# DCN-v2 cross layers on one core: the last round's row blocks stored one by one, the last block's store divided between two queues

## Chip, cores and metric

The kernel runs on one NeuronCore of a Trainium2 chip. The metric is the device time of one execution in microseconds (us). A core has five engines with instruction streams of their own: TensorE (PE; its weight loads are PEld), VectorE (DVE), ScalarE (ACT), GpSimd (POOL) and SyncE (SP), which here does nothing but issue DMA transfers. DMAs are issued by SP and by ScalarE, each into a queue of its own (SPq and ACTq in the profile's rows). KB is 1024 bytes.

## What is computed

Six cross layers over a batch of 4096 rows of 416 features, all in bfloat16:

```python
B, F, D, L = 4096, 26, 16, 6
Din = min(F * D, 1024)          # 416
# x0: [4096, 416], ws: [6, 416, 416], bs: [6, 416]
def reference(x0, ws, bs):
    x = x0
    for l in range(ws.shape[0]):
        x = x0 * (x @ ws[l] + bs[l]) + x
    return x
```

## The kernel before

Every x is x0 times a factor c, with c = 1 at the start and c + (x @ W + b) after each layer. So the kernel keeps c, adds each layer's product to it, and multiplies by x0.

**First five layers.** Activations lie transposed: features on partitions, batch rows along the free dimension. The 416 features are three chunks of 128 (XM0, XH, CM) and a remainder of 32 (XR, CR), the batch two halves `s` of 2048 rows. TensorE multiplies into PSUM tiles (`pt`), ScalarE evicts them with the bias (L187, L333), VectorE adds into CM and multiplies by XM0. In the fifth layer (`feeding_layer`) c is also sent through DMA transposes on SP (L232, L380), so that it lies with batch rows on partitions in XLrows. X0rows is x0 in the same layout; SP loads it early (L131 to L133), behind the weights, in 18 transfers of one or two row blocks each. Four loads of the last bias follow it on SP (L135), and then the transposes.

**Last layer (from L446).** Its product comes out with batch rows on partitions. A *row block* is 128 rows by 416 columns, one PSUM bank of 416 float32 per partition, 104 KB in bfloat16. There are 32 row blocks, worked off in four rounds of eight (`rounds`, L518). In a round a block has a number `u` from 0 to 7. When `mm_q_full` has finished a block or two, `close` calls `ew`. There ScalarE copies the bank to an SBUF tile `t` (L507), and VectorE adds the rows of XLrows (L511). The product with X0rows (L494) and the store wait in the list `pending` until the next block's addition has been put in VectorE's stream; `close_product` then writes the product into an output tile `o` and issues the store. Output tiles hold two blocks and come from a pool of ten (`opool`).

**Last round.** Here blocks are closed one at a time, in order (`ENDS`). `final` is true and three things differ. For u of 5 and more c was added on TensorE with an identity (L468, L470), so that L511 is left out. Block 7 isn't copied by ScalarE either: VectorE's product reads it in PSUM (L494, `o<-py`). And `paired` (L528) decides how blocks share output tiles and stores: blocks 0 to 5 lie two in a tile, `j` being 0 or 1, and each tile is stored when its second block is there (`last`). Blocks 6 and 7 have a tile and a store each. All stores are issued by SP, only block 7's by ScalarE (`eng`, L532).

**What orders the work.** VectorE's instructions and some others are pinned in program order. Each engine runs its stream in order; between engines the framework puts semaphore waits. SP issues its stores in order, each behind a wait for VectorE's product. The end sequence (L577) waits on SP for the stores to land, and then all engines meet at a barrier.

Of the kernel before, what the change touches and what calls it, by code (L numbers as in the profile page):

```python
# [16 lines left out]
def kernel(  # L17
# [7 lines left out]
    nc = tc.nc  # L25
    B, D = x0.shape
    L = ws.shape[0]
    P = 128
# [7 lines left out]
    NBT = B // P  # L36
# [9 lines left out]
    out_v = out.rearrange("(bt p) d -> p bt d", p=P)  # L46
# [26 lines left out]
    def load_wm(eng, l):  # L73
        eng.dma_start(WM[:, l], ws[l, 0:NK * P, :].rearrange("(k p) n -> p k n", p=P))
# [5 lines left out]
    def pin(ins):  # L80
        tc.keep_in_program_order(ins)
# [46 lines left out]
        load_wr(nc.sync, g, 1, L)  # L128
    for l in range(2, L):
        load_wm(nc.sync, l)  # L130
    for q in range(18):  # L131
        b0, b1 = NBT * q // 18, NBT * (q + 1) // 18
        nc.sync.dma_start(X0rows[:, b0:b1, :], x0_v[:, b0:b1, :])  # L133
    for g in range(NG):
        nc.sync.dma_start(bLr[32 * g:32 * g + 1, :], bs[LL:LL + 1, :])  # L135
# [319 lines left out]
    def mm_q_open(q, g, py):  # L455
        for k in range(NK):
            for j in range(0, P, 32):
                nc.tensor.matmul(py[j:j + 32, 0:D], lhsT=q_x(q, g, k)[:, j:j + 32], rhs=WM[:, l, k, :],  # L458
                                 start=(k == 0), stop=False, tile_position=(0, j))

    def mm_q_full(q, g, py, closes, adds=False):
        s, i = quads[q]
        for k in range(NK):
            nc.tensor.matmul(py[:, 0:D], lhsT=q_x(q, g, k), rhs=WM[:, l, k, :],  # L464
                             start=((not closes) and k == 0), stop=(closes and not adds and k == NK - 1))
            if adds:
                c0 = col0(s, g) + 128 * i
                nc.tensor.matmul(py[:, P * k:P * k + P], lhsT=CM[:, k, c0:c0 + 128], rhs=ident[:], start=False, stop=False)  # L468
        if adds:
            nc.tensor.matmul(py[:, NK * P:D], lhsT=CR[:, CW * s + 128 * i:CW * s + 128 * i + 128],  # L470
                             rhs=ident[:, 32 * g:32 * g + 32], start=False, stop=True)

    def mm_q_rem(q, py, done):
        s, i = quads[q]
        biased = s == NS - 1 and i >= 2
        for g in range(NG):
            nc.tensor.matmul(py[g][:, 0:D], lhsT=curR[32 * g:32 * g + 32, CW * s + 128 * i:CW * s + 128 * i + 128],  # L477
                             rhs=WR[32 * g:32 * g + 32, l, :], start=(g >= done), stop=(not biased and g < done),
                             tile_position=(32 * g, 0))
        for g in range(NG if biased else 0):  # L480
            nc.tensor.matmul(py[g][:, 0:D], lhsT=ones[32 * g:32 * g + 1, :],  # L481
                             rhs=bLr[32 * g:32 * g + 1, :], start=False, stop=(g < done), tile_position=(32 * g, 0))

    pending, outs = [], []

    def rows(q, g0, n):
        s, i = quads[q]
        b0 = 16 * s + 4 * g0 + i
        return slice(b0, b0 + 4 * (n - 1) + 1, 4)

    def close_product():
        while pending:
            src, q, g0, n, o, j, last, eng = pending.pop()
            pin(nc.vector.tensor_tensor(out=o[:, j:j + n, :], in0=src, in1=X0rows[:, rows(q, g0, n), :], op=ALU.mult))  # L494
            if last:
                eng.dma_start(out_v[:, rows(q, g0 - j, j + n), :], o[:, 0:j + n, :])

    def ew(q, g0, srcs, o, j, last, eng, added, direct):
        if direct:
            close_product()  # L500
            pending.append((srcs[0], q, g0, 1, o, j, last, eng))
            return
        t = tpool.tile([P, 2 * CW], BF16, name="t")
        n = 0
        for src in srcs:
            w = src.shape[1]
            nc.scalar.copy(t[:, n * D:n * D + w * D].rearrange("p (a d) -> p a d", a=w), src)  # L507
            n += w
        tv = t[:, 0:n * D].rearrange("p (a d) -> p a d", a=n)
        if not added:  # L510
            pin(nc.vector.tensor_tensor(out=tv, in0=tv, in1=XLrows[:, rows(q, g0, n), :], op=ALU.add))  # L511
        close_product()
        pending.append((tv, q, g0, n, o, j, last, eng))
# [5 lines left out]
    for q, at, done in rounds:  # L519
        tiles = [psum.tile([P, 2, CW], FP32, tag="ps", name=f"py{n}") for n in range(4)]  # L520
        bank = [tiles[n][:, a, :] for n, a in at]

        final = q + 2 == NQ

        def close(groups):
            u = groups[0][0]
            srcs = [tiles[at[g[0]][0]][:, at[g[0]][1]:at[g[0]][1] + len(g), 0:D] for g in groups]
            paired = final and u < 6  # L528
            j = u % 2 if paired else 0
            if not j:  # L530
                outs.append(opool.tile([P, 2, D], BF16, name="o"))
            ew(q + u // 4, u % 4, srcs, outs[-1], j, bool(j) or not paired, nc.scalar if final and u == 7 else nc.sync,  # L532
               final and u >= 5, final and u == 7)

        for u in range(done):
            if q == 0:
                mm_q_open(q, u, bank[u])
            else:
                mm_q_full(q, u, bank[u], False)
        mm_q_rem(q, bank[0:4], done)  # L540
        close([range(done)])
        if q == 0:
            last_rows_out()
        mm_q_rem(q + 1, bank[4:8], 0)
        for u in range(done, 8):
            mm_q_full(q + u // 4, u % 4, bank[u], True, final and u >= 5)
            if at is ENDS:
                close([[u]])
            elif u % 2:
                close([[u - 1, u]] if at is PAIRS else [[u - 1], [u]])  # L550
    close_product()


# [28 lines left out]
```

## Time and profile before

| | us |
|---|---|
| median of 3 runs | 128.86 (128.81 to 128.91) |
| the profiled execution's own time | 129.12 |
| its span, first to last instruction | 127.3 |
| TensorE clock granted | 1.000 |
| last layer begins (first L458 in the chain of waits) | 103.6 |
| last matmul (L470) starts | 123.65 |
| product of block 7 on VectorE (L494, from PSUM) | 123.97, lasts 0.58 |

The span leaves out what lies around the program's instructions, so a change of the span stands beside the same change of the time. In the profile's rows "L494 DVE ... o<-t,X0rows 128x416" is an instruction of line 494 on VectorE that writes `o` and reads `t` and `X0rows`; a trailing number after x counts instructions. In the timeline a row of several instructions shows the first one's start and the time until the last one's end. Some rows of the stage around the change:

```profile
L464 PE MATMUL py<-WM,XH 128*128 128x416 bf16 x90 | 17.0, 339 | 0.0
L494 DVE TENSOR_TENSOR o<-t,X0rows 128x832 bf16<-128x832 bf16 x12 | 7.0, 584 | 0.0
L507 ACT CAST t<-py 128x416 bf16<-128x416 f32 x13 | 6.6, 506 | 1.6 <-PE py L481 0.6 <-PE py L464 0.4 <-DVE o L494 0.2
L494 DVE TENSOR_TENSOR o<-t,X0rows 128x416 bf16<-128x416 bf16 x7 | 2.4, 372 | 0.1
L494 DVE TENSOR_TENSOR o<-py,X0rows 128x416 bf16<-128x416 f32 x1 | 0.6, 584 | 0.0
...
out_dram<-o SPq DMA_DIRECT2D x15, 208.0 KB, 2.9
X0rows<-in_x_dram SPq DMA_DIRECT2D x14, 208.0 KB, 4.4
X0rows<-in_x_dram SPq DMA_DIRECT2D x4, 104.0 KB, 5.4
out_dram<-o SPq DMA_DIRECT2D x1, 104.0 KB
```

In the first five rows the two numbers after the bar are busy us of all and mean ns of one, and after the second bar stands the engine's idle time before them. The other rows are DMA issues: how many, KB of each, and the median us from issue to landing.

### The profile page before, as it was taken

Reading aid. Unit: us, or ns where it says so; the run is one execution under the profiler, and the core shown is the slowest. Engines: PE = TensorE matmul, PEld = TensorE weight load, DVE = VectorE, ACT = ScalarE, POOL = GpSimd, SP = SyncE. Lnnn points to the kernel's source line nnn. Section 1 sums busy time; section 2 is a strip of 40 time slices with the busy share of each in tenths; the row PEclk is TensorE's granted clock in tenths of the full one; section 3 lists DMA queues with packets and bytes.
Section 4 is the critical chain, followed back from the end, with each engine's and each line's share of the span. In section 5 each row is a group of like instructions: output and inputs, shape, how many; then the busy total and the mean of one; then the engine's idle time right before and its main releaser. Section 6 shows DMA issues by size and latency. Waiting matters only on the chain.

```text
span 127.3 us, 3951 instructions
## 1 busy us (share of the span) xinstructions
PE 122.9 (97%) x1684; PEld 55.3 (43%) x1686; DVE 102.4 (80%) x192; ACT 88.3 (69%) x113; POOL 5.1 (4%) x18
## 2 busy tenths in 40 slices
PE   7999999999999999999999999999999999999980
PEld 3243343344534443444354445444534445445450
DVE  0033679674989898998898998898999999999991
ACT  0047866896869486869486859485859698679660
POOL 4004001400000000000000000000000000000000
PEclk9999999999999999999999999999999999999999
DMA  3999999999960000000000000000088999999865
GB/s 90 239 222 228 190 242 256 299 332 335 315 192 0 5 0 0 8 0 5 0 5 0 0 5 0 5 0 5 0 83 137 197 150 202 171 256 320 262 198 187
DMA packets 42230, 16.38 MB, mean 129 GB/s; under 512 B 31034, under 2 KB 42212, under 8 KB 42212
## 3 DMA queue, kind: packets, MB, share of 16 engines
q1 hardware_dynamic: 37432, 15.40, 53.3%
q10 hardware_dynamic: 4780, 0.72, 3.7%
q8 instruction: 13, 0.21, 0.7%
q14 instruction: 5, 0.04, 0.1%
HBM read 6.15 MB, written 3.41 MB: 75 GB/s over the span
## 4 chain that ended last, share of the span: by engine, by line
PE 90%; DMA 5%; SPq 1%; DVEq 1%; ACT 0%; issue 0%; DVE 0%
PE pt L209 50%; PE py L464 12%; PE ph L241 11%; DMA XM<-in_x_dram 5%; PE pt L215 5%; PE pr L225 5%; PE pr L221 2%; PE py L477 2%; PE ph L248 1%; SPq L78 1%; PE py L458 1%; DVEq L577 1%; ACT t L507 0%; PE py L481 0%; PE py L468 0%
## 5 line engine op out<-in xcount | busy, mean ns | idle before, releaser
L209 PE MATMUL pt<-XH,WM 128*32 128x512 bf16 x1152 | 65.2, 379 | 0.0
L187 ACT ACTIVATE t<-pt,bM 128x1024 bf16<-128x1024 f32 x36 | 37.2, 1115 | 13.1 <-PE pt L215 13.1
L209 PEld LDWEIGHTS <-WM 128*32 128x32 bf16 x1152 | 29.7, 97 | 33.8 <-issue 5.1
L188 DVE TENSOR_TENSOR CM<-t,CM 128x1024 bf16<-128x1024 bf16 x36 | 24.7, 687 | 4.3 <-ACT t L187 4.3
L189 DVE TENSOR_TENSOR XH<-CM,XM 128x1024 bf16<-128x1024 bf16 x36 | 24.9, 692 | 2.6
L507 ACT CAST t<-py 128x416 bf16<-128x416 f32 (+1 forms) x22 | 14.2, 649 | 4.2 <-PE py L464 2.0
L464 PE MATMUL py<-WM,XH 128*128 128x416 bf16 x90 | 17.0, 339 | 0.0
L241 PE MATMUL ph<-XM,WM 128*128 128x512 bf16 x70 | 16.3, 380 | 0.2
L333 ACT ACTIVATE t<-pt,bM 128x1024 bf16<-128x1024 f32 x12 | 12.4, 1115 | 4.1 <-PE pt L215 4.1
L181 ACT ACTIVATE CM<-ph,bM 128x1024 bf16<-128x1024 f32 x12 | 12.5, 1114 | 3.5 <-PE ph L248 3.5
L183 DVE TENSOR_TENSOR XH<-CM,XM 128x512 bf16<-128x512 bf16 x24 | 8.9, 430 | 4.5 <-ACT CM L181 4.5
L464 PEld LDWEIGHTS <-XH 128*128 128x128 bf16 x90 | 8.5, 98 | 7.5 <-issue 1.2
L241 PEld LDWEIGHTS <-WM 128*128 128x128 bf16 x72 | 6.7, 98 | 8.6 <-issue 1.3
L494 DVE TENSOR_TENSOR o<-t,X0rows 128x832 bf16<-128x832 bf16 (+1 forms) x19 | 9.4, 506 | 0.1
L511 DVE TENSOR_TENSOR t<-t,XLrows 128x832 bf16<-128x832 bf16 (+1 forms) x17 | 8.9, 523 | 0.0
L341 DVE TENSOR_TENSOR CM<-t,CM 128x1024 bf16<-128x1024 bf16 x12 | 8.0, 686 | 0.3 <-ACT t L333 0.3
L345 DVE TENSOR_TENSOR XH<-CM,XM 128x2048 bf16<-128x2048 bf16 (+1 forms) x7 | 7.5, 1068 | 0.2
L215 PE MATMUL pt<-XR,WR 32*128 32x512 bf16 x96 | 7.3, 379 | 0.0
L225 PE MATMUL pr<-XH,WM 128*32 128x512 bf16 x96 | 6.6, 379 | 0.0
L197 ACT ACTIVATE t<-pr,bR 128x256 bf16<-128x256 f32 (+1 forms) x16 | 5.3, 427 | 1.6 <-PE pr L225 1.6
L114 ACT ACT_TABLE_LOAD x1 | 1.3, 1283 | 6.1 <-DMA XM<-in_x_dram 6.1
L157 DVE CAST bM<-pb 128x18 f32<-128x18 bf16 x1 | 0.2, 177 | 5.5 <-PE pb L156 5.5
(61 smaller groups left out, 62.2 us busy)
## 6 DMA issues: line engine op xcount, KB each, us to landing
out_dram<-o SPq DMA_DIRECT2D x15, 208.0 KB, 2.9
X0rows<-in_x_dram SPq DMA_DIRECT2D x14, 208.0 KB, 4.4
WM<-in_ws_dram SPq DMA_DIRECT2D x5, 312.0 KB, 5.7
WR<-in_ws_dram SPq DMA_DIRECT2D x4, 130.0 KB, 3.9
X0rows<-in_x_dram SPq DMA_DIRECT2D x4, 104.0 KB, 5.4
WM<-in_ws_dram ACTq DMA_DIRECT2D x1, 312.0 KB, 3.3
XM<-in_x_dram SPq DMA_TRANSPOSE x8, 5.1
xrig<-in_x_dram ACTq DMA_DIRECT2D x4, 32.0 KB, 4.5
```

The source lines that it names most:

```text
L181: nc.scalar.activation(c, src, ACT.Identity, bias=bias, scale=1.0)
L187: nc.scalar.activation(t[:], src, ACT.Identity, bias=bias, scale=1.0)
L188: nc.vector.tensor_tensor(out=c, in0=t[:], in1=c, op=ALU.add)
L189: nc.vector.tensor_tensor(out=x, in0=c, in1=XM0[:, m, c0:c0 + 2 * CW], op=ALU.mult)
L209: nc.tensor.matmul(pts[g // 2][32 * q:32 * q + 32, g % 2, :], lhsT=WM[:, l, k, 128 * m + 32 * q:128 * m + 32 * q + 32], rhs=cur[s][:, k, C ...
L215: nc.tensor.matmul(pts[g // 2][:, g % 2, :], lhsT=WR[32 * g:32 * g + 32, l, 128 * m:128 * m + 128], rhs=curR[32 * g:32 * g + 32, CW * s:CW ...
L225: nc.tensor.matmul(pr[32 * g:32 * g + 32, :], lhsT=WM[:, l, k, NK * P:D], rhs=cur[s][:, k, CW * g:CW * g + CW], start=False, stop=(k == NK ...
L241: nc.tensor.matmul(pt[:, gl, :], lhsT=WM[:, 0, k, 128 * m:128 * m + 128], rhs=cur[:, k, c0:c0 + CW], start=(k == 0 and not after_row), sto ...
L333: nc.scalar.activation(ts[t + (h,)][:], pts[t][h][:].rearrange("p a b -> p (a b)"), ACT.Identity, bias=bM[:, t[1], l:l + 1], scale=1.0)
L464: nc.tensor.matmul(py[:, 0:D], lhsT=q_x(q, g, k), rhs=WM[:, l, k, :], start=((not closes) and k == 0), stop=(closes and not adds and k == ...
L494: pin(nc.vector.tensor_tensor(out=o[:, j:j + n, :], in0=src, in1=X0rows[:, rows(q, g0, n), :], op=ALU.mult))
L507: nc.scalar.copy(t[:, n * D:n * D + w * D].rearrange("p (a d) -> p a d", a=w), src)
```

## The change

X0rows comes in 15 loads of two or three row blocks (104 KB a block) instead of 18 of one or two. In the last round only blocks 4 and 5 still share a tile and a store; blocks 0 to 3 have a tile and a store each. Block 7's store becomes two: SP issues partitions 0 to 63, ScalarE partitions 64 to 127, 52 KB each. A block with `eng` set to `None` is block 7.

```diff
-    for q in range(18):
-        b0, b1 = NBT * q // 18, NBT * (q + 1) // 18
+    for q in range(15):
+        b0, b1 = NBT * q // 15, NBT * (q + 1) // 15
         nc.sync.dma_start(X0rows[:, b0:b1, :], x0_v[:, b0:b1, :])
...
             pin(nc.vector.tensor_tensor(out=o[:, j:j + n, :], in0=src, in1=X0rows[:, rows(q, g0, n), :], op=ALU.mult))
-            if last:
+            if eng is None:
+                for e, part in ((nc.sync, slice(0, P // 2)), (nc.scalar, slice(P // 2, P))):
+                    e.dma_start(out_v[part, rows(q, g0, 1), :], o[part, 0:1, :])
+            elif last:
                 eng.dma_start(out_v[:, rows(q, g0 - j, j + n), :], o[:, 0:j + n, :])
...
-            paired = final and u < 6
+            paired = final and u in (4, 5)
             j = u % 2 if paired else 0
             if not j:
                 outs.append(opool.tile([P, 2, D], BF16, name="o"))
-            ew(q + u // 4, u % 4, srcs, outs[-1], j, bool(j) or not paired, nc.scalar if final and u == 7 else nc.sync,
+            ew(q + u // 4, u % 4, srcs, outs[-1], j, bool(j) or not paired, None if final and u == 7 else nc.sync,
                final and u >= 5, final and u == 7)
```

## The prediction

> **What bounds the kernel now.** I read the page's engine sums and chain first, then the chain's last pieces, the waits of SP's queue, SP's and ScalarE's timeline of the last microseconds, the DMA issues, and last a table of short stretches from 121 us on.
>
> ```profile
> span 127.3 us, 3951 instructions
> PE 122.9 (97%) x1684; PEld 55.3 (43%) x1686; DVE 102.4 (80%) x192; ACT 88.3 (69%) x113; POOL 5.1 (4%) x18
> ...
> 123.68 0.04 DVE o L494
> 123.72 0.16 issue
> 123.88 0.68 DVEq L577
> ```
>
> TensorE is busy 97% of the span, and the chain is almost all TensorE until 123.1 us. The change touches nothing on TensorE. The listed chain ends at 123.88 + 0.68 = 124.56 us, though the span ends at 127.3: the last 2.7 us belong to something the chain doesn't follow. The waits of SP's queue show what:
>
> ```profile
> SPq L577 <- DMA out_dram<-o: 1.8, 4, 0.6
> ...
> 123.07 0.94 SPq L496 DMA_DIRECT2D out_dram<-o  x2
> 123.64 0.90 SPq L496 DMA_DIRECT2D out_dram<-o  x2
> ...
> 124.59 0.38 ACTq L496 DMA_DIRECT2D out_dram<-o  x1
> ...
> out_dram<-o ACTq DMA_DIRECT2D x1, 104.0 KB, 1.9
> DMA to landing us min/median/max: 1.9/2.7/3.6
> ```
>
> At its end (L577) SP waits four times for stores. The last store, ScalarE's 104 KB, is issued at 124.59 and lands 1.9 us later, at 126.5; the end sequence takes the other 0.8 us to 127.3. So the end is the landing of the last store, and only what moves that landing counts. Here is what the DMA engines do then (last two columns: busy share of the 16 engines, GB/s):
>
> ```profile
> 122.40:122.60 0.20, 0.20 (x3) 0.15 (x2) 0.20 (x2) 0.13 (x1) 0.00 (x0) 1.00 0.10 25
> 122.60:122.80 0.20, 0.20 (x4) 0.15 (x2) 0.20 (x2) 0.20 (x1) 0.00 (x0) 1.00 0.07 21
> 122.80:123.00 0.20, 0.20 (x6) 0.12 (x3) 0.20 (x2) 0.18 (x1) 0.00 (x0) 1.00 0.79 266
> ...
> 123.60:123.80 0.20, 0.20 (x3) 0.09 (x1) 0.13 (x2) 0.05 (x1) 0.00 (x0) 1.00 0.00 0
> 123.80:124.00 0.20, 0.03 (x2) 0.00 (x0) 0.20 (x2) 0.00 (x0) 0.00 (x0) 1.00 0.10 29
> 124.00:124.20 0.20, 0.00 (x0) 0.00 (x0) 0.20 (x2) 0.00 (x0) 0.00 (x0) 1.00 0.93 300
> ...
> 125.80:126.00 0.20, 0.00 (x0) 0.00 (x0) 0.00 (x0) 0.00 (x0) 0.00 (x0) 1.00 0.91 283
> 126.00:126.20 0.20, 0.00 (x0) 0.00 (x0) 0.00 (x0) 0.00 (x0) 0.00 (x0) 1.00 0.40 112
> ```
>
> The engines idle from 122.4 to 122.8 and from 123.5 to 123.96, and are then full until about 126.07 (112 GB/s in the last slice is 22 KB, 0.07 us at the full rate). In that full stretch go the pair issued at 123.07, the pair issued at 123.64, the single store of 124.11 and ScalarE's of 124.59: 208 + 208 + 104 + 104 KB, 639,000 bytes in 2.11 us, 303 GB/s. The tail is bound by transfer rate, after a gap in which the engines had nothing.
>
> **Part 1, X0rows in 15 loads instead of 18.** It removes three issues of SP at a median of 0.43 us (L133's row), 1.3 us of SP's time between 22.8 and 34.7 us. Behind them on SP stand four small bias loads and then nothing until 93.08: one wait of SP there lasts 58.5 us. The bytes are the same; the first reader of X0rows is L494 at 109.1 us, the longest landing 5.4 us after the issue. Even without that cover of some 70 us the price would be of the sign of a gain. Zero.
>
> **Part 2, blocks 0 to 3 stored singly.** SP issues four stores for two, 2 × 0.37 us more. Products of these blocks begin at 120.96, 121.53, 122.10 and 122.67 and last 0.37; a store was issued 0.03 after its product (121.90 to 121.93). So the issues go to 121.37, 121.93, 122.51 and 123.07: each lasts about 0.4 in a spacing of 0.57, so SP still is free for the pair (4, 5) at 123.64, block 6 at 124.11 and the last at 124.59. What changes is the bytes' time: data starts 0.89 us after an issue when the engines are free (121.93 to 122.82, 123.07 to 123.96). Block 2 then moves at 123.40 to 123.74 instead of behind 123.96; block 3 at 123.96 to 124.30.
>
> From there: the pair (4, 5) can't start before 123.64 + 0.89 = 124.53, with the engines empty. Behind it stand 208 + 104 + 104 KB, 426,000 bytes: 1.41 us at 303 GB/s, ending at 125.94, or 1.35 us at the 316 GB/s of a full slice, ending at 125.88. Against 126.07 that is a gain of **0.13 to 0.19 us**. It isn't the whole 0.34 us that block 2's 104 KB takes, since the engines now idle from 124.30 to 124.53.
>
> The four single stores also use four output tiles for two, seven in the round instead of five, out of ten that go round. VectorE's product must wait until the tile's former store landed. The last block's tile was last stored by the stage's ninth store, issued at 118.01 and landed by 118.01 + 3.6 = 121.6 at most; its product starts at 123.97. Cover 2.4 us, price zero.
>
> **Part 3, the last block's store in halves.** SP issues partitions 0 to 63, ScalarE 64 to 127. ScalarE's issue stays at 124.59. SP's half queues behind block 6's issue, which ends at 123.64 + 0.90 = 124.54, and behind its wait for the same product: 124.59. Behind it on SP stands only the end sequence. An issue of 128 rows took 0.38; four one-row issues (bLr) took 1.25, 0.31 each with gaps. So the half's issue lies between these, at most 0.07 us better. Whether data starts sooner for it no row shows: 0 to 0.07, and I take 0, since data began 0.89 after the issue of 256 rows too.
>
> The rate of two halves isn't in the trace. The best case is that together they run like one store, 106,500 bytes at 310 GB/s, 0.34 us. The worst is that each runs like a load confined to few partitions. The nearest such row are the four WR loads, 32 partitions and 130 KB each:
>
> ```profile
> 20.30:22.90 2.60, 2.55 (x15) 1.16 (x13) 2.05 (x7) 2.57 (x3) 1.14 (x2) 1.00 1.09 220
> 24.00:25.00 1.00, 1.00 (x15) 0.24 (x17) 1.00 (x3) 0.60 (x2) 0.65 (x2) 1.00 1.11 321
> ```
>
> Full engines moved 220 GB/s while these went, 321 GB/s for the X0rows loads over 128 partitions. At 220 the block takes 0.48 us, 0.14 more. I take no loss in full, because both halves are in flight at once and between them cover all partitions, but keep to the low end of the gain. The Trainium skill speaks against the split: "DMA: Bandwidth & Descriptors", section "Rules for kernel authors", says that two transfers to disjoint partition halves share the same 16 engines and serialize, and advises one transfer; "SBUF — State Buffer", section "Door 1: The DMA port swizzle", says that partitions 0 to 63 reach no more ports than 0 to 31. By these the 220 row holds for each half and the change ends at no gain. The WR row agrees about few partitions; no run here shows two halves at once.
>
> **Sum.** −0 − 0.13 ± 0 = −0.13 us: the profiled span 127.3 (its own time 129.12) would be 127.2. The median of the runs is 128.86, 0.26 below the profiled execution; a change in the tail carries over as it is: **128.73 us**, its own range 128.55 to 128.90. The best case sets the floor: data of the last store not before 124.59 + 0.89 = 125.48, done 0.34 later at 125.82, a gain of 0.25; with the shorter issue 0.32.
>
> **Rivals.** (a) *The halves cost what the single stores gain*: 0.13 − 0.14, **128.87 us**. For it the WR row; against it that the halves overlap in time. (b) *The last store meets empty engines and the shorter issues count*: 0.32, **128.54 us**. For it the idle gaps before 124 us; against it the sum of bytes, which keeps the engines full until block 6 is through at 125.5 or later. (c) *The slower side: block 6's issue on SP grows and the half queues behind it.* SP's issues of stores last 372 to 1209 ns. At 1.21 the half is issued at 125.36, data starts at 126.25, and 52 KB at 220 to 310 GB/s end at about 126.45 instead of 126.07: +0.38, **129.24 us**. It decides from an issue of some 0.8 us on, below that the half is ready in time. For it that SP now issues seven times in the last 3.2 us, against it that the long issues stood in the crowd of stores after 112 us, 208 KB every 0.55 us, more than the engines move; now it is 104 KB every 0.57, about 190 GB/s, and issues near the end took 0.37 to 0.43. (d) *The end is set by fixed latency alone*: 1.9 us is the least landing time of all stores, perhaps it can't be less, **128.86 us**. Against it the full engines right up to 126.0.
>
> **How the numbers follow.** Forecast 0.43, (a) 0.15, (b) 0.16, (c) 0.18, (d) 0.08. Less than 0.2%, 0.26 us, is about what a measurement can't tell from no change: faster means below 128.60. That is (b), and some 0.07 of the forecast's own spread: 0.23. Slower, above 129.12, is most of (c): 0.16. The same: 0.61. The range 128.50 to 129.10 takes in the forecast, (a), (d), most of (b) and the milder forms of (c); about 0.1 is left out on each side.
>
> **What would show it.** Right: stores on SP near 121.4, 121.9, 122.5, 123.1; DMA share above 0 between 123.4 and 123.7; the full stretch starting near 124.5; the last landing near 126.4. Part 3 wrong: the share or the rate falls to about 220 GB/s after 125.5. Rival (c): an SP issue over 0.8 us after 124 us. The prediction is wrong as a whole if the product of the last block no longer starts near 123.97, since then VectorE or TensorE was disturbed, which I cost at nothing.

## The result and the profile after

The changed kernel takes 129.24 us, the median of 8 runs (129.13 to 129.59), against 128.84 us (128.72 to 129.08, 8 runs). The ratio is 1.0032, 95% interval 1.0021 to 1.0043: slower by 0.41 us, 0.27 to 0.55.

The profiled spans, 127.4 and 127.3 us, don't show this by themselves. The profiled execution of before, 129.12 us, lay 0.28 above its median: it came to block 7's product 0.32 us later than that of the changed kernel, a difference that goes back to its first matmuls. So tails are compared, from the start of block 7's product to the last landing: 123.97 to 126.51, **2.53 us** by the unrounded times, before; 123.65 to 126.53, **2.88 us**, after. From the last landing to the end both take 0.83. The tail is 0.34 us longer; the rest, up to 0.41, is within the interval.

The timeline of block 7's product and its two stores after the change (start, length, engine, line):

```profile
123.65 0.58 DVE L494 TENSOR_TENSOR o<-py,X0rows 128x416 bf16<-128x416 f32 x1
...
124.27 0.56 ACTq L497 DMA_DIRECT2D out_dram<-o  x1
124.30 0.55 SPq L497 DMA_DIRECT2D out_dram<-o  x1
```

Both halves are issued where one store was, right behind the product, but each issue lasts 0.55 to 0.56 us; before, the whole store's took 0.38. The same kernel's DMA issues (count, KB, us to landing):

```profile
out_dram<-o ACTq DMA_DIRECT2D x1, 52.0 KB, 2.0
out_dram<-o SPq DMA_DIRECT2D x1, 52.0 KB, 2.2
```

Half the bytes take longer to land than the whole had, 1.9 us. And its short stretches, 0.2 us each (last two columns: busy share of the DMA engines, GB/s):

```profile
125.00:125.20 0.20, 0.00 (x0) 0.00 (x0) 0.00 (x0) 0.00 (x0) 0.00 (x0) 1.00 0.98 333
125.20:125.40 0.20, 0.00 (x0) 0.00 (x0) 0.00 (x0) 0.00 (x0) 0.00 (x0) 1.00 0.25 75
125.40:125.60 0.20, 0.00 (x0) 0.00 (x0) 0.00 (x0) 0.00 (x0) 0.00 (x0) 1.00 0.43 92
125.60:125.80 0.20, 0.00 (x0) 0.00 (x0) 0.00 (x0) 0.00 (x0) 0.00 (x0) 1.00 0.84 179
125.80:126.00 0.20, 0.00 (x0) 0.00 (x0) 0.00 (x0) 0.00 (x0) 0.00 (x0) 1.00 0.91 200
```

Three things stand here. The older stores are through by about 125.3: the single stores did empty the engines earlier, as forecast. Then there is a hole: by the trace's packets ScalarE's half starts at 125.48, 1.21 us after its issue, and SP's at 125.75, 1.45 after its issue, when ScalarE's, which ends at 125.90, is nearly through. And at a share of 0.84 to 0.91 they move only 179 to 200 GB/s; their packets last 59 and 65 ns in the median, against 42 before. The tail is no longer bound by the older stores' bytes but by the halves themselves.

### The profile page after: what moved, and what is told of

Same layout as the page of the kernel before. It is cut to its first block, busy times and chain, and to the rows that moved or that the text cites. A ratio compares the mean times of both kernels' runs of the same rounds, so it can differ in the third digit from the quotient of the medians.

```text
span 127.4 us, 3955 instructions
## 1 busy us (share of the span) xinstructions
PE 122.2 (96%) x1684; PEld 55.3 (43%) x1686; DVE 102.6 (81%) x192; ACT 88.2 (69%) x113; POOL 4.6 (4%) x18
## 4 chain that ended last, share of the span: by engine, by line
PE 90%; DMA 4%; ACTq 2%; DVEq 1%; issue 0%; ACT 0%; DVE 0%
PE pt L209 50%; PE py L464 12%; PE ph L241 11%; PE pt L215 5%; PE pr L225 5%; DMA xrig<-in_x_dram 4%; PE pr L221 2%; PE py L477 2%; PE ph L248 1%; PE py L458 1%; ACTq L86 1%; DVEq L580 1%; ACTq L108 1%; ACT t L510 0%; PE tpr L163 0%
## 5 line engine op out<-in xcount | busy, mean ns | idle before, releaser
L209 PEld LDWEIGHTS <-WM 128*32 128x32 bf16 x1152 | 29.7, 97 | 33.8 <-issue 5.1
L225 PEld LDWEIGHTS <-WM 128*32 128x32 bf16 x120 | 3.2, 97 | 3.2
```

The costliest lines, as they stand in the source:

```text
L209: nc.tensor.matmul(pts[g // 2][32 * q:32 * q + 32, g % 2, :], lhsT=WM[:, l, k, 128 * m + 32 * q:128 * m + 32 * q + 32], rhs=cur[s][:, k, C ...
L225: nc.tensor.matmul(pr[32 * g:32 * g + 32, :], lhsT=WM[:, l, k, NK * P:D], rhs=cur[s][:, k, CW * g:CW * g + CW], start=False, stop=(k == NK ...
```

## The experiments

Each experiment's ratio is against the kernel before, run on the same chip, whose median was 128.90 to 128.93 us in these comparisons. The ratio is worked out from all runs and can differ from that of the medians, by up to 0.12% here (e6). "Tail" is as above; "end" is from the last landing to the span's end; both come from one profile each. Before, e3 and e10 have the same stores, and their tails agree within 0.01 us.

| | us | ratio (95%) | tail | end |
|---|---|---|---|---|
| before | 128.84 | 1 | 2.53 | 0.83 |
| after | 129.24 | 1.0032 (1.0021 to 1.0043) | 2.88 | 0.83 |
| e1, single stores, last store whole, 15 loads | 128.82 | 0.9994 (0.9985 to 1.0003) | 2.42 | 0.90 |
| e2, halves alone, pairs, 18 loads | 129.31 | 1.0033 (1.0020 to 1.0045) | 2.89 | 0.93 |
| e3, 15 loads alone | 129.18 | 1.0019 (1.0010 to 1.0029) | 2.53 | 1.03 |
| e4, after, both halves on ScalarE | 129.82 | 1.0077 (1.0064 to 1.0090) | 3.37 | 0.83 |
| e5, after, halves by columns | 128.83 | 1.0004 (0.9994 to 1.0013) | 2.52 | 0.83 |
| e6, all stores single and whole, 15 loads | 128.97 | 1.0017 (1.0006 to 1.0028) | 2.65 | 0.84 |
| e7, before with 10 loads | 129.54 | 1.0052 (1.0039 to 1.0064) | 3.23 | 0.83 |
| e8, e1 with 16 loads | 128.71 | 0.9990 (0.9981 to 0.9999) | 2.41 | 0.84 |
| e9, after, halves by even and odd partitions | 129.19 | 1.0020 (1.0010 to 1.0030) | 2.79 | 0.89 |
| e10, before with 26 loads | 128.97 | 1.0003 (0.9993 to 1.0012) | 2.53 | 0.84 |

### Which part is the loss (e1, e2, e3)

e1, against the changed kernel:

```diff
-    bool(j) or not paired, None if final and u == 7 else nc.sync,
+    bool(j) or not paired, nc.scalar if final and u == 7 else nc.sync,
```

> Blocks 0 to 3 stored singly and X0rows in 15 loads as in the changed kernel, block 7's store undivided on ScalarE as before. Theory H (the divided store is the loss, the single stores are a gain): block 7's product starts with the DMA engines nearly empty of older stores, its data starts about 0.9 us after its issue, lands about 1.75 us after it instead of 1.9, and the time is 0.1 to 0.25 us below before, 128.6 to 128.75. Rival S (the single stores are the loss, through five more small stores or the output tiles that they use): the time stays at 129.1 or above.

e2, against the changed kernel:

```diff
-    for q in range(15):        # and // 15 below
+    for q in range(18):        # and // 18 below
-            paired = final and u in (4, 5)
+            paired = final and u < 6
```

> Only block 7's store is divided; pairs and 18 loads as before. Theory H: both issues near 0.55 us, ScalarE's half starts to move 1.2 us after the issue, SP's half 0.25 later, the last landing about 2.2 us after the issue instead of 1.9; +0.3 to +0.5 us, 129.15 to 129.35. Rival S: no slower than before, 128.8.

e3 is the kernel before with 15 for 18 in the X0rows loop.

> Only X0rows in 15 loads. Both theories: no change, 128.84 within 0.1 us; the landings of X0rows come later than 4.4 us after the issue but some 70 us ahead of their first reader. If it is more than 0.15 us slower, the loss lies in the loads after all.

With the store whole, the single stores shorten the tail by 0.11 us and the time shows no loss, so rival S falls. The halves alone lengthen the tail by 0.35, as much as the change does. (The time of e2 also has 0.10 in its longer end, which theory W below accounts for.) In the changed kernel both together give 2.88, no better than the halves alone: the halves start late enough for the older stores to be through in either case (by 125.47 in e2, where the first half starts at 125.50), so the earlier bytes buy nothing.

e3 missed both theories: 0.24 us slower, with the tail of before. What grew is the end, 0.83 to 1.03. The end sequence's waits on SP, first in the kernel before and then in e3 (length min/median/max, first and last start):

```profile
L577 SPq EVENT_SEMAPHORE  x7: 17/28/28, 124.6 to 127.3; - x7
```

```profile
L577 SPq EVENT_SEMAPHORE  x7: 17/28/28, 126.1 to 127.4; - x7
```

The DMAs use eight semaphores in turn, and the end sequence waits for them in a fixed order, in five instructions. Before, these passed at 124.59, 125.19, 125.87, 126.19 and 126.53: the last store was waited for last, and the others had been ticked off meanwhile. Three DMAs fewer turn the wheel by three: in e3 the first wait passed only at 126.12, the last store's at 126.46, and three more followed at 126.52, 126.59 and 126.65. That is 0.06 us each, 0.2 us together. (Call this theory W.) In the change itself three loads less and three stores more keep the last store in its place. e2 has one DMA more than before and e1 one less: two waits follow the last store's in e2 and one in e1, and their ends are 0.10 and 0.07 us longer.

### What is slow about the halves (e4, e5, e9)

```diff
-                for e, part in ((nc.sync, slice(0, P // 2)), (nc.scalar, slice(P // 2, P))):
+                for e, part in ((nc.scalar, slice(0, P // 2)), (nc.scalar, slice(P // 2, P))):
```

> The changed kernel with both halves issued by ScalarE, one behind the other, so that no two issues coincide. If the meeting of two issues is what costs (theory H1): each issue back to about 0.35 us, the first half starts to move 0.9 us after its issue, the second 0.4 later, last landing about 2.0 after the first issue: 0.2 us faster than the changed kernel, 129.05. If a store of 64 partitions is slow in itself (theory H2): the first half starts 1.2 us after its issue as in the changed kernel, its packets last 60 ns and more, and the time is 129.2 or above. Rates near 200 GB/s after 125 us are expected by both.

The short stretches of e4:

```profile
125.40:125.60 0.20, 0.00 (x0) 0.00 (x0) 0.00 (x0) 0.00 (x0) 0.00 (x0) 1.00 0.12 33
125.60:125.80 0.20, 0.00 (x0) 0.00 (x0) 0.00 (x0) 0.00 (x0) 0.00 (x0) 1.00 0.79 171
...
126.40:126.60 0.20, 0.00 (x0) 0.00 (x0) 0.00 (x0) 0.00 (x0) 0.00 (x0) 1.00 0.74 171
```

The issues, at 124.42 and 125.27, met no other and still lasted 0.52 and 0.48 us. Data came 1.2 and 1.1 us after them, at 171 GB/s. So H2 holds: a store of 64 partitions is slow in itself, without a second one beside it. Why ScalarE began the second issue 0.32 us after the first was over isn't settled.

```diff
-                for e, part in ((nc.sync, slice(0, P // 2)), (nc.scalar, slice(P // 2, P))):
-                    e.dma_start(out_v[part, rows(q, g0, 1), :], o[part, 0:1, :])
+                for e, part in ((nc.sync, slice(0, D // 2)), (nc.scalar, slice(D // 2, D))):
+                    e.dma_start(out_v[:, rows(q, g0, 1), part], o[:, 0:1, part])
```

> The changed kernel with block 7's store divided by columns: SP 208 columns, ScalarE 208 columns, each over all 128 partitions in rows of 416 bytes. If few partitions are what makes the halves slow (theory P): issues near 0.38 us, data 0.9 us after the issue, no 200 GB/s stretch, last landing about 1.8 us after the issue instead of 2.2: 128.75, as with single stores and an undivided last block. If two stores at the end cost whatever their shape (theory T): 129.1 or above. Rows of 416 bytes may cost something of their own, up to 0.2 us.

```diff
-                for e, part in ((nc.sync, slice(0, P // 2)), (nc.scalar, slice(P // 2, P))):
+                for e, part in ((nc.sync, slice(0, P, 2)), (nc.scalar, slice(1, P, 2))):
```

> The changed kernel with block 7's store divided by even partitions (SP) and odd partitions (ScalarE), 64 partitions each, spread over the whole range. If the place of the partitions is what slows the halves (theory P1): no stretch of 60 ns packets near 200 GB/s after 125 us, last landing about 1.9 us after the issue, 128.8. If it is their number, 64 rows in one DMA (theory P2): issue 0.55 us and data 1.2 us after it as in the changed kernel, though the packets may be quick: 129.0 to 129.2.

The stores of e5 and then of e9 in their timelines:

```profile
124.28 0.39 ACTq L497 DMA_DIRECT2D out_dram<-o  x1
124.31 0.40 SPq L497 DMA_DIRECT2D out_dram<-o  x1
```

```profile
124.49 0.59 ACTq L497 DMA_DIRECT2D out_dram<-o  x1
124.52 0.56 SPq L497 DMA_DIRECT2D out_dram<-o  x1
```

The landings in e5's DMA issues:

```profile
out_dram<-o ACTq DMA_DIRECT2D x1, 52.0 KB, 1.7
out_dram<-o SPq DMA_DIRECT2D x1, 52.0 KB, 1.9
```

and e9's short stretches:

```profile
125.60:125.80 0.20, 0.00 (x0) 0.00 (x0) 0.00 (x0) 0.00 (x0) 0.00 (x0) 1.00 0.25 75
125.80:126.00 0.20, 0.00 (x0) 0.00 (x0) 0.00 (x0) 0.00 (x0) 0.00 (x0) 1.00 0.67 204
126.00:126.20 0.20, 0.00 (x0) 0.00 (x0) 0.00 (x0) 0.00 (x0) 0.00 (x0) 1.00 0.74 233
```

Cut by columns, over all 128 partitions, the halves' issues are back at 0.39 and 0.40 us though they coincide, and the tail is 2.52. Cut into even and odd partitions they stay slow: issues of 0.56 and 0.59, data 1.20 us after SP's issue, as expected under P2, and ScalarE's only after SP's, 1.51 after its issue. Only the packets recover, 40 ns in the median: 204 GB/s at a share of 0.67 is 304 at a full one, where the changed kernel's 200 at 0.91 is 220. So the cut into 64 partitions sets the issue and the start, and the place of the partitions the rate. What in the cut does it isn't separated: a half of 64 partitions also has 64 packets, one of e5 has 128. From the tails: whole store 2.41 (e8); two stores by columns +0.11; 64 rows each instead of 128 +0.27 (e9); in two blocks of neighbouring partitions +0.08 more (after). Together 0.46 us. Single profiles stand behind these, so the split is good to some hundredths.

### The count of DMAs, and a better version (e6, e7, e8, e10)

e6 sets `paired = False` in e1. e7 and e10 are the kernel before with 10 and 26 in place of 18; e8 is e1 with 16 in place of 15.

> Blocks 4 and 5 stored singly too, block 7 undivided on ScalarE, X0rows in 15 loads. That is one DMA more than the first experiment, so the last store again lands on the semaphore that the end sequence waits for last. If the order of these waits matters (theory W): from the last landing to the end 0.83 us as before, not 0.91. Block 4's 104 KB goes 0.25 us earlier, so the last store meets free engines: landing 1.75 us after its issue. Together 128.6 to 128.7. If W is wrong: 128.8.

> The kernel before with X0rows in 10 loads, 8 fewer than 18. The DMAs' semaphores go round by eight, so the last store comes back to the semaphore that is waited for last. Theory W: the time of before, within 0.1 us; last landing to end 0.83 us. Rival B (bigger and fewer loads cost the 0.25 us that 15 loads alone cost): 129.2 or more, since the loads are bigger still.

> The first experiment (single stores, undivided last block) with 16 loads of X0rows instead of 15, one DMA more, so that the last store lands on the semaphore waited for last. Theory W: last landing to end 0.83 us instead of 0.91, time 0.05 to 0.1 below the first experiment, 0.13 to 0.2 below before. Rival B: as the first experiment.

> The kernel before with X0rows in 26 loads, eight more than 18, so that the last store again lands on the semaphore waited for last. Theory W with the instruction fetch (SP fetches a block of instructions at a fixed place of its stream, which 10 loads moved into the last stores): the fetch comes four stores earlier than in the kernel before, near 117 us, and costs nothing there; last landing to end 0.83 us; the time of before within 0.1 us, 128.9. Rival B (any number of loads other than 18 costs something by itself): 129.1 or more.

e8 came out as theory W had it: the end fell from 0.90 to 0.84, the time to 128.71, 0.10% (0.01 to 0.19) below before. Its short stretches and its last store:

```profile
125.40:125.60 0.20, 0.00 (x0) 0.00 (x0) 0.00 (x0) 0.00 (x0) 0.00 (x0) 1.00 0.84 262
125.60:125.80 0.20, 0.00 (x0) 0.00 (x0) 0.00 (x0) 0.00 (x0) 0.00 (x0) 1.00 0.02 4
```

```profile
out_dram<-o ACTq DMA_DIRECT2D x1, 104.0 KB, 1.8
```

The product starts at 123.60, in the changed kernel at 123.65, and the data is out by 125.64 instead of 126.17. This version beats both kernels, if by little.

e6 missed. Its end was 0.84, as W expects, but its tail 2.65. SP issues single stores that are ready no faster than one in 0.46 to 0.49 us (here at 123.21, 123.69 and 124.19), and the products of blocks 4 to 7 begin 0.28 to 0.44 apart. Block 6's store went at 124.19 instead of 123.74 and block 7's landed behind it, 2.04 us after its issue. The pair of blocks 4 and 5 spares SP the issue that it has no time for.

e7 missed too, in a way that neither theory had: its end is the 0.83 of W, but its tail is 3.23. SP's timeline:

```profile
123.36 1.25 SPq L496 DMA_DIRECT2D out_dram<-o  x2
```

Block 6's product was there at 123.77, but SP began the store only at 124.26: its previous issue ended at 123.73, and its next instruction, a wait for a store long landed, came at 124.17. This pause isn't peculiar to e7. In the kernel before, e2, e7, e8 and e10, SP's 80th traced instruction, each time a wait for a store long landed, begins 0.44 to 0.47 us after the end of the one before it; the waits of this kind around it follow within 0.06. In every run an instruction fetch of 8 KB on one DMA engine comes when SP has begun 80 to 84 of its traced instructions: at 121.3 us in the kernel before, at 122.0 in the changed one, at 125.3 in e7. Eight loads fewer put that place four stores later, among the last. e10 shifts it the other way, to 118.3, with the last store waited for last again, and the time is that of before. So rival B falls, and W holds for e3, e8 and e10.

The pause itself is the smaller part of e7's loss. The trace has 16 signals for the landing of a store: 15 of the last store's had come by 126.30, 2.61 us after block 7's product began, against 2.53 for all of them in the kernel before; the sixteenth came at 126.92. Eight packets of the last store, a sixteenth of its 128, ran on to 126.37 when the others were out by 125.93. Meanwhile instruction fetches held a DMA engine for 0.31 us from 125.30 and 0.35 us from 125.90 (every run has one near its end, like the second). So some 0.08 us go with the pause and 0.63 with one late part of the store. That the fetches made it late fits the times, but the profile doesn't tell which engine a packet used, and it wasn't tried alone.

## Why the prediction was wrong

The time came out 0.51 us above the forecast of 128.73. The halves, which the sum put at nothing, cost 0.46 us of tail.

**What bounds the kernel**: right. In all runs the differences lay in the way from block 7's product to the last landing, or in the end sequence behind it (0.83 to 1.03 us).

**Part 1, no cost for the loads**: right for the change, wrong as argued. The bytes and SP's time early on are indeed hidden, but the count of DMAs decides which semaphore the last store signals: 0.2 us in e3. The change was spared because it adds as many stores as it removes loads.

**Part 2, 0.13 to 0.19 us gained by the single stores**: right, at its low end. The issues came at 121.25, 121.71, 122.18 and 122.75; with the 0.32 us by which this profile is ahead the last two are where they were expected, the first two 0.2 and 0.1 late, without consequence (the first is SP's 80th traced instruction, where the pause seen in e7 lies). The tail shrank by 0.11 to 0.12 (e1, e8), the time of e8 by 0.13 (0.01 to 0.24). By the packets the data of before ends at 126.14, not at 126.07 as the prediction read from the slices, and that of e8 0.12 us earlier, counted from block 7's product.

**Part 3, the halves at nothing**: this is the step that failed. The prediction put the half's issue between 0.31 and 0.38 us, by rows of one and of 128 partitions, and the start of its data at 0.89 us after the issue, by stores of two blocks. A half measured 0.55 and 1.2 (1.45 for the second one): its price lay outside the two rows that were to bound it. The rate of 220 GB/s that the WR row showed, kept as the bad end at 0.14 us, was right for the halves in their blocks of partitions, but only 0.08 of the 0.46 us that the division costs. "Both halves are in flight at once" was wrong in the main: ScalarE's moved from 125.48 to 125.90 and SP's from 125.75 to 126.17, together for 0.14 us only. The Trainium skill, "DMA: Bandwidth & Descriptors", section "Rules for kernel authors", says that two transfers to disjoint partition halves serialize; this trace agrees but for those 0.14 us. For partitions 0 to 63 the Trainium skill, "SBUF — State Buffer", section "Door 1: The DMA port swizzle", gives about 218 GB/s as the limit for large transfers; the 179 to 200 GB/s of the changed kernel lie below it.

**The rivals.** (a) named the right part, by its rate alone, with less than a third of its price. (c) named the measured 129.24 us, by a mechanism that didn't occur: block 6's issue lasted 0.42 us and SP's half was issued 0.03 after ScalarE's. That its number came true is chance. What (c) feared, SP short of time for its issues, did appear in e6. (b) didn't occur: even in e8 older stores moved until 125.30, when the last store's data had begun at 125.13, and the tail shrank by 0.12 us of (b)'s 0.32. (d) falls: 1.8 and 1.7 us were reached.

## What to carry to other kernels

When the end of a kernel is one store's landing, move the bytes in front of it earlier, and leave that store whole over all 128 partitions: dividing it bought no time in any of the four ways tried here and cost 0.1 to 0.95 us of tail against e8. Bound the cost of a new shape by a row of that shape; rows on both sides of it were no bounds here. Before a count of DMAs is changed anywhere, see which wait of the end sequence the last store releases and what SP does at the end of its stream: three loads fewer at about 30 us made this kernel 0.24 us longer, eight fewer 0.67.

## What the runs showed of the hardware

A store of 64 partitions took 0.48 to 0.59 us to issue and began to move 1.1 to 1.2 us after that issue's start, the second of two issued at once 1.45 to 1.5 us. The last round's stores of 128 partitions took 0.33 to 0.5 to issue, and the last one began at 0.9 (e1, e8) to 1.1 us (e6). Where the 64 partitions lay made no difference to the issue and the first start, nor did a second issue at the same time (after, e4, e9). It is no rule for few partitions: ScalarE's load of 32 partitions into WR, 26 KB, took 0.33 us to issue (before, after). SP's end sequence took 0.06 us for every wait behind the one that the last store releases. SP paused for 0.44 us at a fixed place of its stream, and an instruction fetch, 8 KB on one DMA engine for 0.3 to 0.55 us, followed 0.7 to 1.6 us after the pause (before, e2, e7, e8, e10).
